# A block-sparse attention and feed-forward kernel: where the first weight matrix lies raw, in which order the two matrices are decoded, which queue carries the later transfers, and how many gathers go out at a time

## The chip, the cores and the metric

The kernel runs on one core of one Trainium2 chip. The metric is the device time of one execution in microseconds (us); less is better. The engines named below are PE (TensorE), DVE (VectorE), ACT (ScalarE), POOL (GpSimd) and SP (SyncE, which here only starts transfers). Transfers started by SP, ACT and POOL stand in three queues, q1, q10 and q0, and are carried out by the core's 16 DMA engines.

## The reference, cut to what matters

```python
# q, k, v: (4 batches, 8 heads, 768 positions, 64); 24 blocks of 32 positions
scores = np.matmul(q, k.transpose(0, 1, 3, 2)) / np.sqrt(64)
# a query block sees: its neighbours (|i - j| <= 1), the first and the last block,
# 3 sampled blocks of its own; blocks 0 and 23 see everything
attn = softmax(np.where(mask, scores, -1e9)) @ v
x = attn.transpose(0, 2, 1, 3).reshape(3072, 512)
h = x @ w_in                                   # w_in: 512 x 2048, float64
sp = np.maximum(h, 0) + np.log1p(np.exp(-np.abs(h)))
out = (h * erf(sp)) @ w_out                    # w_out: 2048 x 512, float64
```

The weights arrive as float64. The kernel takes them as pairs of 32-bit words and makes float32 of them on DVE.

## The kernel before, in words

**Work units.** Each of the four batches has 16 attention units: ten "m" units (five groups of four query blocks, two halves of the heads each), four "f" and two "e" units for the edge blocks. A unit is: `scores` on PE into `s`; `soft_max` (maximum, on DVE, into `mx` and `nb`); `soft_exp` (exponentials and a rounded copy on ACT, into `pf` and `p`); `soft_low` (the rest `p` on DVE); `soft_turn` (transposes of `p` into `pT`, on PE in the prologue, by a DMA transpose of SP's queue later). Two units later `values` multiplies `pT` with the value rows in `vb` on PE (into `po`), `norm` divides on DVE (into `xf`) and `turn` makes the transposed feed-forward input `xT`.

**Feed-forward steps.** The main loop has 96 groups plus a lag of two. Step m does on PE `ff_first` of group m (`h`, 24 products with `w_in`), `values`, `scores`, and `ff_second` of group m-2 (`o`, 12 products with `w_out`); on ACT five logarithm and exponential passes over `h` (`ff_logs`: four names `x`, one `q`), one more later (`ff_exp`); on DVE `ff_gate` of group m-1 (`q`, `g`, `g`) and `ff_power`. Each engine runs its instructions in the order in which the program writes them.

**Weights.** `w_in` and `w_out` are 16 raw pieces of 512 KB each. `load_weight` starts a transfer; step D (`decode_pair`) turns two pieces into float32 with three DVE instructions through `spare_k`; Q (`square_pair`) sums squares on ACT; A and B (`sum_w`, `scale_w`) make a scale from all eight sums of a matrix; H and L (`split_hi` on ACT, `split_lo` on DVE) make the two float16 halves which PE uses. "Di4" is D of pair 4 of `w_in`, "Lo0" L of pair 0 of `w_out`. A group of `ff_first` uses two pairs (steps 0 and 1 pairs 0 and 1, steps 2 and 3 pairs 2 and 3, and so on); `ff_second` of group n uses pair n of `w_out`. Raw pieces lie in the matrix's own tile, in slots that decoding frees step by step, and the last two in `spare_k`. The strings in `WEIGHTS` give what the main loop does at the end of steps 0, 1, 2 and so on.

**Values.** `load_v` brings raw `v`, `split_v` makes two float16 halves and writes them to a table in DRAM (`vtab`); `gather_v` brings the rows that two query blocks see into two of the eight slots of `vb`, some nine to twelve small transfers of SP's queue, and `gathers` starts as many as there are free slots. Before `values` of the first unit, SP's queue has: raw k, q, v; weights; the four writes to `vtab`; then the gathers. `gather` copies key blocks on POOL (`kg`).

**Queues.** SP's queue carries everything of the first batch, all gathers and DMA transposes and the q loads; POOL's carries the other weight pieces; ACT's the k and v of later batches and the results (`write_results`).

Of the kernel before, what the change touches and what calls it, by code (L numbers as in the profile page):

```python
# [26 lines left out]
WEIGHTS = (  # L27
    "Do7 Qo7 Hi2 Li2 Ao/Hi3 Li3 Bo Ho0 Lo0/Hi4 Li4 Ho1 Lo1/Hi5 Li5 Ho2 Lo2"
    "/Hi6 Li6 Ho3 Lo3/Hi7 Li7 Ho4 Lo4/Ho5 Lo5/Ho6 Lo6/Ho7 Lo7"
# [5 lines left out]
def sparse_attention_moe(ctx: ExitStack, tc: tile.TileContext, qT, kT, v, sampled, w_in, w_out, out):  # L35
# [36 lines left out]
    FF_LAG = 2  # L72
# [27 lines left out]
    def load_k(b, pr):  # L100
# [8 lines left out]
        eng = sp if b == 0 else act  # L109
        eng.dma_start(kr, kT[b, 2 * pr : 2 * pr + 2].rearrange("t d s -> (t d) s"))  # L110
# [38 lines left out]
    def load_v(b, quad):  # L149
# [5 lines left out]
        eng = act if b else sp  # L155
        eng.dma_start(vr, v[b][:, quad * 4 : quad * 4 + 4].rearrange("p h k d -> p h (k d)"))
# [185 lines left out]
    numbers = {}  # L342
# [15 lines left out]
    def gather_v(b, first):  # L358

        rows, last = vtab[b], first + 2  # L360
        if first % 4 == 1:
            numbers[b] = block_numbers(first, min(first + 4, NB - 1), SYNC)
# [67 lines left out]
    def raw_slot(i):  # L430

        return 2 + 2 * i if i < 8 else 10 + 2 * (i - 8) if i < 12 else 14 + 2 * (i - 12)
# [3 lines left out]
    def load_weight(eng, key, i):  # L436

        raw = spare_k[:, (i - 14) * 1024 : (i - 13) * 1024] if i > 13 else slots(wmats[key][0], raw_slot(i), 2)
# [5 lines left out]
        eng.dma_start(raw, rows)  # L444

    def decode_pair(key, k):

        t = wmats[key][0]
        raw = spare_k[:, :2048] if k == 7 else slots(t, raw_slot(2 * k), 4)
        decode(t, (2 * k + 2) * 512, raw, wide)  # L450
# [33 lines left out]
    wsteps = iter(WEIGHTS.split("/"))  # L484
# [261 lines left out]
    def write_results():  # L746
        for result in results:
            act.dma_start(*result)
# [15 lines left out]
    def gathers(m):  # L764

        nonlocal kfree, vfree
        if kjobs and kfree >= 4 and kjobs[0][0] in have_k:
            kfree -= 4
            gather(*kjobs.pop(0))
        while vjobs and vjobs[0][0] in have_v:  # L770
            b, i = vjobs[0]
            n = 2 if i > 0 else 1
            if vfree < n:
                break
            vfree -= n
            vjobs.pop(0)
            gather_v(b, i) if i > 0 else whole_v(b, -1 - i)

    def next_queries(m):

        b, n = divmod(m, per)
        if n < 10 and n % 2 == 1:
            order_q(b, n // 2 + 1)
        if n == per - 1 and b + 1 < B:
            order_q(b + 1, 0)

    def behind(m):

        b, n = divmod(m, per)
        if n < 10 and n % 2 == 0 and (b > 0 or n > 4):  # L790
            load_q(b, n // 2 + 1)
        if b + 1 < B:
            c = b + 1
            if n == 10:
                load_q(c, 0)
            if b == 0:
# [15 lines left out]
            if 7 <= n < 11:  # L812
                order_k(c, n - 7)
            if 6 <= n < 10:
# [222 lines left out]
```

## Time and profile before

| | |
|---|---|
| runs of the kernel before | 879.27, 879.34, 880.84 us; median 879.34 us |
| the profiled execution's own time | 874.48 us |
| its span, first to last instruction | 872.7 us |
| PE busy | 713.5 us, 82% of the span |
| ACT busy | 601.1 us, 69% |
| DVE busy | 555.3 us, 64% |
| POOL busy | 122.6 us, 14% |
| mean granted PE clock | 0.932 of full speed |

The profiled execution is one execution; its time is 4.86 us under the median of the three others, and 1.8 us of it lie outside the span. A busy share is an average over stages: the first hundred microseconds, the steps in which weights are split, and the rest have different limits.

### The profile page before, as it was taken

Reading aid. Unit: us, or ns where it says so; the run is one execution under the profiler, and the core shown is the slowest. Engines: PE = TensorE matmul, PEld = TensorE weight load, DVE = VectorE, ACT = ScalarE, POOL = GpSimd, SP = SyncE. Lnnn points to the kernel's source line nnn. Section 1 sums busy time; section 2 is a strip of 40 time slices with the busy share of each in tenths; the row PEclk is TensorE's granted clock in tenths of the full one; section 3 lists DMA queues with packets and bytes.
Section 4 is the critical chain, followed back from the end, with each engine's and each line's share of the span. In section 5 each row is a group of like instructions: output and inputs, shape, how many; then the busy total and the mean of one; then the engine's idle time right before and its main releaser. Section 6 shows DMA issues by size and latency. Waiting matters only on the chain. (4 is left out here: it accounts for less than half of the span.)

```text
span 872.7 us, 26694 instructions
## 1 busy us (share of the span) xinstructions
PE 713.5 (82%) x11100; PEld 510.1 (58%) x11100; DVE 555.3 (64%) x974; ACT 601.1 (69%) x999; POOL 122.6 (14%) x346
## 2 busy tenths in 40 slices
PE   1324357669994989899988999799989999999997
PEld 1213245446673667666766776566767676667664
DVE  3946866677763666865665677765656677655443
ACT  4634557778774767786775778776757686876774
POOL 6502120101210203200011121200111000000000
PEclk9965587879997999999999999899999999999999
DMA  8978723667577877962478678941475578221000
GB/s 330 352 216 237 222 66 79 168 177 188 153 153 191 178 172 203 226 176 50 104 198 184 141 178 207 231 95 32 121 193 118 137 159 180 78 50 37 2 26 25
DMA packets 199930, 131.61 MB, mean 151 GB/s; under 512 B 144000, under 2 KB 167168, under 8 KB 199808
## 3 DMA queue, kind: packets, MB, share of 16 engines
q1 hardware_dynamic: 189552, 98.96, 48.5%
q10 hardware_dynamic: 6544, 18.09, 6.5%
q0 software_dynamic: 3712, 12.85, 4.2%
q8 instruction: 87, 1.43, 0.7%
q14 instruction: 35, 0.29, 0.1%
HBM read 83.88 MB, written 12.95 MB: 111 GB/s over the span
## 5 line engine op out<-in xcount | busy, mean ns | idle before, releaser
L51 PE MATMUL h<-xT,wi 128*128 128x256 f16 x2304 | 276.4, 277 | 22.0 <-ACT wi L51 16.9
L51 PE MATMUL o<-wo,g 128*128 128x512 f16 x1152 | 267.4, 381 | 6.2 <-DVE wo L51 4.4
L51 PEld LDWEIGHTS <-wi 128*128 128x128 f16 x2304 | 228.5, 100 | 73.8 <-ACT wi L51 17.9
L51 ACT ACTIVATE x<-x 128x512 f32<-128x512 f32 x288 | 181.5, 630 | 9.1
L51 PEld LDWEIGHTS <-g 128*128 128x128 f16 x1152 | 109.3, 98 | 129.4 <-issue 9.6
L51 POOL COPY kg<-kx 128x128 f32 x264 | 87.1, 379 | 398.0 <-PE s_m L51 310.3
L51 ACT ACTIVATE pf_m<-s_m,nb_m 128x256 f32<-128x256 f32 x160 | 62.6, 474 | 75.0 <-DVE nb_m L51 69.8
L51 DVE SCALAR_TENSOR_TENSOR q<-x,q 128x512 f32<-128x512 f32 x96 | 66.2, 689 | 72.7 <-ACT x L51 71.6
L51 ACT ACTIVATE x<-h,isg 128x512 f32<-128x512 f32 x96 | 65.1, 678 | 52.7 <-PE h L51 33.4
L51 PE MATMUL po<-vb,pT_m 128*32 128x65 f16 (+1 forms) x3840 | 45.4, 206 | 51.9 <-DMA pT_m<-p_m 30.5
L51 PE MATMUL s_m<-kx,qm 128*64 128x64 f32 (+1 forms) x1280 | 76.4, 255 | 10.5 <-ACT pf_m L51 6.9
L51 ACT ACTIVATE q<-q 128x512 f32<-128x512 f32 x96 | 59.5, 620 | 29.9 <-DVE q L51 29.9
L51 DVE SCALAR_TENSOR_TENSOR q<-q,h 128x512 f32<-128x512 f32 x96 | 65.5, 682 | 22.6 <-ACT q L51 22.6
L51 PEld LDWEIGHTS <-pT_m 128*32 128x32 f16 x3840 | 39.4, 101 | 62.1 <-DMA pT_m<-p_m 33.0
L51 DVE TENSOR_TENSOR p_m<-pf_m,p_m 128x1024 f16<-128x1024 f32 x40 | 49.0, 1225 | 37.5 <-ACT p_m L51 37.5
L51 PEld LDWEIGHTS s_m<-kx,qm 128*64 128x64 f32 x1280 | 61.0, 152 | 14.4 <-ACT pf_m L51 7.8
L51 DVE SCALAR_TENSOR_TENSOR g<-q,g 128x512 f16<-128x512 f32 x96 | 66.5, 692 | 3.3
L51 DVE TENSOR_REDUCE mx_m<-s_m 128x4 f32<-128x1024 f32 x40 | 48.7, 1219 | 24.8 <-PE s_m L51 24.8
L51 ACT ACTIVATE q<-x 128x512 f32<-128x512 f32 x96 | 60.5, 630 | 3.0
L51 DVE TENSOR_TENSOR x<-xf,x 128x512 f16<-128x512 f32 x24 | 16.7, 696 | 44.9 <-ACT x L51 41.0
L51 PE MATMUL s_m<-kg,qm 128*64 128x96 f32 x640 | 44.8, 265 | 0.0
L51 DVE TENSOR_SCALAR g<-q 128x512 f16<-128x512 f32 x96 | 41.5, 432 | 3.3
(111 smaller groups left out, 629.5 us busy)
## 6 DMA issues: line engine op xcount, KB each, us to landing
vb<-vtab SPq DMA_DIRECT2D x280, 65.0 KB, 2.8
vb<-vtab SPq DMA_DIRECT2D x32, 390.0 KB, 3.9
wo<-in_w_out_dram POOLq DMA_DIRECT2D x14, 512.0 KB, 11.2
vraw<-in_v_dram ACTq DMA_DIRECT2D x9, 768.0 KB, 5.0
vtab<-vn SPq DMA_DIRECT2D x16, 390.0 KB, 4.5
vb<-vtab SPq DMA_DIRECT2D x12, 520.0 KB, 5.0
qt<-in_qT_dram SPq DMA_DIRECT2D x20, 256.0 KB, 4.3
out_dram<-wo ACTq DMA_DIRECT2D x20, 256.0 KB, 3.1
```

Of the source, the lines that this page charges most:

```text
L51: done = call(*args, **kwargs)
```

## The change: what it does

The raw pieces 8 to 15 of `w_in` go to `w_out`'s tile, slots 2 to 17, so they wait for no decoding. SP's queue takes four pieces of `w_in` in place of eight, and POOL's takes the other twelve and two of `w_out` in one go, behind the first key gather. `w_in` is decoded whole before `w_out`; the pieces of `w_out` are asked for as `w_in`'s decoding frees their slots. Four decodings of `w_out` (Do4 to Do7) now stand in the main loop, where one (Do7) stood. The weight steps of the main loop are split over two places, `EARLY` ahead of `ff_second` and `soft_max`, `LATE` at the step's end. k, v and results go through SP's queue. A call of `gathers` takes slots up to a sum of four, where a slot that also needs its edge blocks counts twice. The q loads and the key work of the next batch stand at other steps.

```diff
-WEIGHTS = (
-    "Do7 Qo7 Hi2 Li2 Ao/Hi3 Li3 Bo Ho0 Lo0/Hi4 Li4 Ho1 Lo1/Hi5 Li5 Ho2 Lo2"
-    "/Hi6 Li6 Ho3 Lo3/Hi7 Li7 Ho4 Lo4/Ho5 Lo5/Ho6 Lo6/Ho7 Lo7"
+EARLY = ("Hi2 Li2", "Li3 Qo5", "Ao Bo Ho0 Lo0", "Hi5 Li5", "Hi6 Li6", "Hi7 Li7")
+LATE = (
+    "Hi3 Do4 Qo4 Do5", "Do6 Qo6 Do7 Qo7", "Hi4 Li4 Ho1 Lo1", "Ho2 Lo2",
+    "Ho3 Lo3", "Ho4 Lo4", "Ho5 Lo5", "Ho6 Lo6", "Ho7 Lo7",
 )
...
-        eng = sp if b == 0 else act
-        eng.dma_start(kr, kT[b, 2 * pr : 2 * pr + 2].rearrange("t d s -> (t d) s"))
+        sp.dma_start(kr, kT[b, 2 * pr : 2 * pr + 2].rearrange("t d s -> (t d) s"))
...
-        eng = act if b else sp
-        eng.dma_start(vr, v[b][:, quad * 4 : quad * 4 + 4].rearrange("p h k d -> p h (k d)"))
+        sp.dma_start(vr, v[b][:, quad * 4 : quad * 4 + 4].rearrange("p h k d -> p h (k d)"))
...
+    def raw_of(key, i, n):
+
+        if key == "i":
+            return slots(wi, 2 + 2 * i, 2 * n) if i < 8 else slots(wo, 2 + 2 * (i - 8), 2 * n)
+        if i > 13:
+            return spare_k[:, (i - 14) * 1024 : (i - 14 + n) * 1024]
+        return slots(wo, 2 + 2 * i if i < 8 else 10 + 2 * (i - 8) if i < 12 else 14 + 2 * (i - 12), 2 * n)
...
-        for i in {2: (8, 9), 3: (10, 11), 5: (12, 13)}.get(k, ()):
-            load_weight(pool, key, i)
-        if k == 7 and key == "i":
-            for i in (14, 15):
-                load_weight(pool, "o", i)
+        freed = {4: (0, 1), 5: (2, 3), 6: (4, 5), 7: (6, 7)} if key == "i" else {2: (8, 9), 3: (10, 11), 5: (12, 13)}
+        for i in freed.get(k, ()):
+            load_weight(pool, "o", i)
...
-            act.dma_start(*result)
+            sp.dma_start(*result)
...
+        room = 4 if begun > 0 else VGS
         while vjobs and vjobs[0][0] in have_v:
             b, i = vjobs[0]
             n = 2 if i > 0 else 1
-            if vfree < n:
+            fresh = b > 0 and 0 < i < VGS
+            if vfree < n or room < n * (1 + fresh):
                 break
             vfree -= n
+            room -= n * (1 + fresh)
...
-    for i in range(8):
+    for i in range(4):
         load_weight(sp, "i", i)
...
     gathers(0)
+    numbers[0] = block_numbers(1, 5, SYNC)
+    early.append((0, 1))
+    for i in range(4, 16):
+        load_weight(pool, "i", i)
     for i in (14, 15):
-        load_weight(pool, "i", i)
-    for i in range(8):
         load_weight(pool, "o", i)
...
-    work("Do0 Qo0 Do1 Qo1")
+    work("Di4 Qi4 Di5")
     soft_max(units[2])
     soft_exp(units[2])
-    work("Di4 Qi4")
+    work("Qi5 Di6")
     values_of(seen(units[0]))
     norm(*seen(units[0]))
-    work("Di5 Qi5")
     soft_low(units[2])
 
     soft_turn(units[2])
+    values_of(seen(units[1]))
     scores(units[3])
     used_keys(units[3])
-    work("Do2 Qo2")
+    gathers(0)
+    work("Qi6 Di7 Qi7")
+    norm(*seen(units[1]))
+    work("Do0")
+    turn(*seen(units[1]))
     soft_max(units[3])
+    work("Ai")
     soft_exp(units[3])
     order_q(0, 2)
-    values_of(seen(units[1]))
-    gathers(0)
-    norm(*seen(units[1]))
-    turn(*seen(units[1]))
-    work("Di6 Qi6 Di7")
+    work("Qo0 Do1 Bi Hi0 Qo1")
     soft_low(units[3])
-    work("Qi7")
 
     soft_turn(units[3])
-    work("Do3 Qo3 Ai Do4")
+    work("Li0 Do2 Hi1")
     values_of(seen(units[2]))
-    work("Bi Hi0 Qo4")
     norm(*seen(units[2]))
     values_of(seen(units[3]))
-    work("Do5 Qo5")
+    work("Qo2 Li1")
     norm(*seen(units[3]))
     turn(*seen(units[3]))
-    work("Li0 Hi1 Li1 Do6 Qo6")
+    work("Do3 Qo3")
...
         write_values()
+        write_results()
...
-        if m >= FF_LAG:
-            for u in range(CT):
-                ff_second(*groups[m - FF_LAG], u)
         if last:
             ff_gate(*last)
         if place:
             norm(*place)
+        if m < len(EARLY):
+            work(EARLY[m])
+        if m >= FF_LAG:
+            for u in range(CT):
+                ff_second(*groups[m - FF_LAG], u)
...
-        write_results()
-        work(next(wsteps, ""))
+        if m < len(LATE):
+            work(LATE[m])
```

Where the order on an engine changes, the rows of the two programs show it. The first place is POOL's queue behind the first key gather (`kg_4` is its last copy); before:

```order
L51 COPY kg_4_212<-kx_162 128x128
L51 DMA spare_k<-in_w_in_dram 128x1024 x2
L51 DMA wo<-in_w_out_dram 128x1024 x8
L314 TENSOR_LOAD samp
L51 ISA
L51 COPY kg_5_447<-kx_162 128x128
```

and of the change:

```order
L52 COPY kg_4_208<-kx_158 128x128
L52 DMA wi<-in_w_in_dram 128x1024 x4
L52 DMA wo<-in_w_in_dram 128x1024 x8
L52 DMA spare_k<-in_w_out_dram 128x1024 x2
L313 TENSOR_LOAD samp
L52 ISA
L52 COPY kg_5_384<-kx_158 128x128
```

Fourteen loads of 512 KB stand there where ten stood, and the next key gather (`kg_5`) stands behind all of them.

The second place is DVE in steps 0 and 1 of the main loop, from the maximum of the unit of step 0 on; before (the three rows with `spare_k` are the decoding Do7, the row `wi<-wi,s_wi` is Li2):

```order
L51 TENSOR_REDUCE mx_m_2_0_1350<-s_m_2_0_1325 128x4
L51 TENSOR_SCALAR nb_m_2_0_1352<-mx_m_2_0_1350 128x4
L51 SCALAR_TENSOR_TENSOR q_0_0_1322<-x_0_0_1318,q_0_0_1322 128x512
L51 TENSOR_TENSOR p_m_2_0_1360<-pf_m_2_0_1355,p_m_2_0_1360 128x4x256
L51 TENSOR_SCALAR spare_k<-spare_k 128x1024
L51 SCALAR_TENSOR_TENSOR spare_k<-spare_k 128x1024
L51 SCALAR_TENSOR_TENSOR wo<-spare_k 128x1024
L51 SCALAR_TENSOR_TENSOR wi<-wi,s_wi 128x2x512
L51 TENSOR_REDUCE top_wo<-sums 128x1
L51 SCALAR_TENSOR_TENSOR q_0_0_1322<-q_0_0_1322,h_0_0_1293 128x512
```

and of the change (the six rows with `spare_k` are Do4 and Do5; the last row is Li3):

```order
L52 TENSOR_TENSOR p_m_2_0_1345<-pf_m_2_0_1340,p_m_2_0_1345 128x4x256
L52 TENSOR_SCALAR spare_k<-wo 128x1024
L52 SCALAR_TENSOR_TENSOR spare_k<-wo,spare_k 128x1024
L52 SCALAR_TENSOR_TENSOR wo<-wo,spare_k 128x1024
L52 TENSOR_SCALAR spare_k<-wo 128x1024
L52 SCALAR_TENSOR_TENSOR spare_k<-wo,spare_k 128x1024
L52 SCALAR_TENSOR_TENSOR wo<-wo,spare_k 128x1024
L52 SCALAR_TENSOR_TENSOR q_0_0_1305<-q_0_0_1305,h_0_0_1276 128x512
L52 TENSOR_SCALAR g_0_0_1420<-q_0_0_1305 128x512
L52 SCALAR_TENSOR_TENSOR g_0_0_1420<-q_0_0_1305,g_0_0_1420 128x512
L52 SCALAR_TENSOR_TENSOR wi<-wi,s_wi 128x2x512
```

Two decodings stand between the unit's last DVE instruction and the gate of group 0, where one stood, and the split that PE needs for step 2 (Li3) stands behind the gate.

The third place is SP's queue in the second step of the second batch (`xT_2` and `pT_m_0_1` are transposes of that step, `pT_m_1_0` one of the next step); before, from the last of thirty gather transfers on:

```order
L51 DMA vb<-vtab_95 32x1040
L51 DMA_TRANSPOSE xT_2_2819<-x_0_5_3841 128x8x128
L51 DMA_TRANSPOSE pT_m_0_1_3846<-p_m_0_1_3838 128x16x128
L51 DMA_TRANSPOSE pT_m_1_0_4080<-p_m_1_0_4076 128x16x128
L51 DMA qt_2_4082<-in_qT_dram 128x4x128
```

and of the change, from the last of nine on:

```order
L52 DMA vb<-vtab_95 32x1040
L52 DMA qt_2_3787<-in_qT_dram 128x4x128
L52 DMA_TRANSPOSE xT_2_2819<-x_0_5_3798 128x8x128
L52 DMA_TRANSPOSE pT_m_0_1_3803<-p_m_0_1_3795 128x16x128
L52 DMA vraw_0_3808<-in_v_dram 128x1536
L313 TENSOR_LOAD samp
L52 DMA vb<-vtab_95 32x2x1040 x2
```

The transposes of the step stand behind nine gather transfers and a q load, where thirty stood; nine more gathers, and twelve after these, follow in the next two steps, and a v load stands among them.

## Rows read from the trace of the kernel before

**Rows 1.** SP's queue in order of time, first 180 us: start, us from the first to the last of the run, what, how many.

```profile
5.92 9.43 SPq L51 DMA_DIRECT2D wi<-in_w_in_dram  x8
...
20.23 19.82 SPq L51 DMA_DIRECT2D vtab<-vn  x4
53.51 55.08 SPq L51 DMA_DIRECT2D vb<-vtab  x66
```

**Rows 2.** POOL in order of time, the starts of weight loads, same columns.

```profile
17.28 1.10 POOL L51 DMA_DIRECT2D spare_k<-in_w_in_dram  x2
...
38.31 1.07 POOL L51 DMA_DIRECT2D wi<-in_w_in_dram  x2
41.56 1.04 POOL L51 DMA_DIRECT2D wi<-in_w_in_dram  x2 [2.18 <-DVE wi L51]
```

**Rows 3.** The transfer queues (q1 is SP's, q0 POOL's) in three stretches, 20 to 25, 30 to 35 and 40 to 45 us: packets, MB, time of the packets as a share of 16 engines.

```profile
q0 software_dynamic: 212, 0.80, 40.1%
...
q0 software_dynamic: 488, 1.76, 87.0%
q1 hardware_dynamic: 487, 0.24, 16.2%
...
q1 hardware_dynamic: 1031, 0.52, 98.5%
q0 software_dynamic: 63, 0.25, 23.8%
```

**Rows 4.** DVE in order of time: start, us, what; in brackets the idle time before it and what ended it. The first three are one decoding.

```profile
23.80 0.69 DVE L51 TENSOR_SCALAR spare_k<-wi 128x1024 int32<-128x1024 int32 x1
24.52 1.23 DVE L51 SCALAR_TENSOR_TENSOR spare_k<-wi,spare_k 128x1024 int32<-128x1024 int32 x1
25.78 1.22 DVE L51 SCALAR_TENSOR_TENSOR wi<-wi,spare_k 128x1024 int32<-128x1024 int32 x1
...
66.68 0.16 DVE L51 TENSOR_SCALAR rinv<-po 128x4 f32<-128x4 f32 x1 [13.33 <-PE po L51]
...
154.79 1.21 DVE L51 TENSOR_REDUCE mx_m<-s_m 128x4 f32<-128x1024 f32 x1
...
161.77 1.28 DVE L51 SCALAR_TENSOR_TENSOR wi<-wi,s_wi 128x1024 f16<-128x1024 f32 x1
```

**Rows 5.** PE in order of time, same columns: the end of the first value product, the first product of the first step, the first use of `w_out`, and two waits for the splits of `w_in`.

```profile
65.21 1.44 PE L51 MATMUL po<-vb,pT_m 128*32 128x65 f16 x89 [0.15 <-DMA vb<-vtab]
...
107.45 1.87 PE L51 MATMUL h<-xT,wi 128*128 128x256 f16 x8 [1.11 <-ACT xT L51]
...
143.88 2.76 PE L51 MATMUL o<-wo,g 128*128 128x512 f16 x12
...
161.09 0.61 PE L51 MATMUL h<-xT,wi 128*128 128x256 f16 x2 [5.58 <-ACT wi L51]
...
186.87 0.61 PE L51 MATMUL h<-xT,wi 128*128 128x256 f16 x2 [5.91 <-ACT wi L51]
```

**Rows 6.** ACT in order of time: the first pass over `h` in steps 3 and 5 of the main loop.

```profile
152.48 0.67 ACT L51 ACTIVATE x<-h,isg 128x512 f32<-128x512 f32 x1
...
177.81 0.67 ACT L51 ACTIVATE x<-h,isg 128x512 f32<-128x512 f32 x1
```

**Rows 7.** Stretches of 20 us: busy time of PE, PE's weight loads, DVE, ACT and POOL (instructions in brackets), granted PE clock, DMA share, GB/s.

```profile
140.00:160.00 20.00, 15.50 (x344) 11.21 (x342) 13.07 (x23) 16.96 (x30) 3.93 (x13) 0.93 0.49 113
160.00:180.00 20.00, 17.51 (x354) 12.48 (x355) 14.37 (x21) 14.27 (x23) 1.75 (x6) 0.85 0.65 152
180.00:200.00 20.00, 12.68 (x161) 8.25 (x160) 14.34 (x28) 14.62 (x23) 0.12 (x1) 0.74 0.62 173
260.00:280.00 20.00, 8.99 (x222) 6.88 (x208) 7.89 (x14) 10.56 (x20) 0.00 (x0) 0.80 0.85 212
```

**Rows 8.** SP's queue in order of time at the changes from the first to the second batch and from the second to the third.

```profile
251.56 21.58 SPq L51 DMA_DIRECT2D vb<-vtab  x30
...
274.59 3.97 SPq L51 DMA_TRANSPOSE pT_m<-p_m  x2
...
433.25 20.24 SPq L51 DMA_DIRECT2D vb<-vtab  x27
```

**Rows 9.** PE in order of time, same columns as rows 5: its waits for a DMA transpose.

```profile
278.60 1.50 PE L51 MATMUL po<-vb,pT_m 128*32 128x65 f16 x96 [11.01 <-DMA pT_m<-p_m]
...
352.99 0.96 PE L51 MATMUL po<-vb,pT_m 128*32 128x65 f16 x96 [2.96 <-DMA pT_m<-p_m]
...
459.13 1.18 PE L51 MATMUL po<-vb,pT_m 128*32 128x65 f16 x96 [4.04 <-DMA pT_m<-p_m]
...
557.45 1.50 PE L51 MATMUL po<-vb,pT_m 128*32 128x65 f16 x96 [4.92 <-DMA pT_m<-p_m]
...
647.33 1.51 PE L51 MATMUL po<-vb,pT_m 128*32 128x65 f16 x96 [3.26 <-DMA pT_m<-p_m]
```

**Rows 10.** Transfers over the whole span, by what they write and read: engine, how many, KB each, median us from issue to landing.

```profile
vraw<-in_v_dram ACTq DMA_DIRECT2D x9, 768.0 KB, 5.0
vtab<-vn SPq DMA_DIRECT2D x16, 390.0 KB, 4.5
...
out_dram<-wo ACTq DMA_DIRECT2D x20, 256.0 KB, 3.1
wi<-in_kT_dram ACTq DMA_DIRECT2D x12, 384.0 KB, 3.6
```

More of the change, by code (lines that the diff above doesn't have):

```diff
@@ L341, in sparse_attention_moe @@
     ended = {}
-    numbers = {}
+    numbers, early = {}, []
     def whole_rows(b):
@@ L360, in gather_v @@
         rows, last = vtab[b], first + 2
-        if first % 4 == 1:
+        if first % 4 == 1 and (b, first) not in early:
             numbers[b] = block_numbers(first, min(first + 4, NB - 1), SYNC)
@@ L428, in sparse_attention_moe @@
     wide = spare_k[:, 2048:3072]
-    def raw_slot(i):
-        return 2 + 2 * i if i < 8 else 10 + 2 * (i - 8) if i < 12 else 14 + 2 * (i - 12)
+    def raw_of(key, i, n):
[4 more added lines that the diff above has]
+        return slots(wo, 2 + 2 * i if i < 8 else 10 + 2 * (i - 8) if i < 12 else 14 + 2 * (i - 12), 2 * n)
     assert NK * NG == NF == 16
     def load_weight(eng, key, i):
-        raw = spare_k[:, (i - 14) * 1024 : (i - 13) * 1024] if i > 13 else slots(wmats[key][0], raw_slot(i), 2)
         if key == "i":
@@ L443, in load_weight @@
             rows = w_out[i * P : (i + 1) * P, :].bitcast(I32)
-        eng.dma_start(raw, rows)
+        eng.dma_start(raw_of(key, i, 1), rows)
     def decode_pair(key, k):
         t = wmats[key][0]
-        raw = spare_k[:, :2048] if k == 7 else slots(t, raw_slot(2 * k), 4)
-        decode(t, (2 * k + 2) * 512, raw, wide)
-        for i in {2: (8, 9), 3: (10, 11), 5: (12, 13)}.get(k, ()):
-            load_weight(pool, key, i)
-        if k == 7 and key == "i":
-            for i in (14, 15):
-                load_weight(pool, "o", i)
+        decode(t, (2 * k + 2) * 512, raw_of(key, 2 * k, 2), wide)
+        freed = {4: (0, 1), 5: (2, 3), 6: (4, 5), 7: (6, 7)} if key == "i" else {2: (8, 9), 3: (10, 11), 5: (12, 13)}
+        for i in freed.get(k, ()):
+            load_weight(pool, "o", i)
     def square_pair(key, k):
@@ L483, in sparse_attention_moe @@
     steps_of = {"D": decode_pair, "Q": square_pair, "A": sum_w, "B": scale_w, "H": split_hi, "L": split_lo}
-    wsteps = iter(WEIGHTS.split("/"))
     def work(steps):
@@ L783, in next_queries @@
             order_q(b, n // 2 + 1)
+            if n < 9:
+                load_q(b, n // 2 + 2)
         if n == per - 1 and b + 1 < B:
             order_q(b + 1, 0)
+            load_q(b + 1, 1)
     def behind(m):
         b, n = divmod(m, per)
-        if n < 10 and n % 2 == 0 and (b > 0 or n > 4):
-            load_q(b, n // 2 + 1)
         if b + 1 < B:
@@ L795, in behind @@
                 load_q(c, 0)
+            k = n if b else 2 * (n - 10) if n > 9 else -1
+            if k in ((1, 3, 5, 7) if b else (2, 4, 6, 8)):
+                order_k(c, (k - 1) // 2)
+            if k in (0, 2, 4, 6):
+                load_k(c, k // 2)
+            if k == 8:
+                have_k.add(c)
             if b == 0:
@@ L811, in behind @@
                 have_v.add(c)
-            if 7 <= n < 11:
-                order_k(c, n - 7)
-            if 6 <= n < 10:
-                load_k(c, n - 6)
-            if n == 10:
-                have_k.add(c)
     def seen(unit):
@@ L996, in sparse_attention_moe @@
             soft_turn(unit)
-        write_results()
-        work(next(wsteps, ""))
+        if m < len(LATE):
+            work(LATE[m])
         if unit:
             behind(begun - 1)
+    write_results()
 _OUTS = [((3072, 512), "float32")]
```

1 line of the change is left out of this document (removed).

## The prediction

> **What bounds the kernel now.** I read the busy times by stage first, then each engine in order of time in the first 200 us, then PE's waits after that. Averages hide three stages.
>
> The first stage ends when PE starts the feed-forward, at 107.45 us [rows 5]. It is a chain of transfers and then of DVE work. SP issues the four writes to `vtab` from 20.23 us on and is done with that at 40.05, but its first gather starts only at 53.51 [rows 1]: it waits for the last write to land. The first value product ends at 66.65 [rows 5], and DVE, which has decoded ahead until 53.35, sits idle for 13.33 us until then [rows 4]. From 66.65 on DVE works off decodings. One decoding is 0.69 + 1.23 + 1.22 = 3.14 us [rows 4], and seven stand between the first value product and the first `h` (Di5, Do2, Di6, Di7, Do3, Do4, Do5).
>
> The second stage, steps 0 to 8, ends near 200 us. PE waits 5.58 and 5.91 us there for splits of `w_in` that stand at the end of the step before [rows 5]. ACT and DVE are far from idle in it: from 140 to 200 us ACT is busy 16.96 + 14.27 + 14.62 = 45.9 of 60 us, DVE 41.8 [rows 7].
>
> In the third stage PE sets the pace and loses time where a DMA transpose comes late: 11.01 us at 278.60, and 2.96, 4.04, 4.92 and 3.26 us later [rows 9]. At the first, SP had issued thirty gathers for 21.58 us and came to the transposes at 273 to 275 us [rows 8].
>
> **The change, part by part.** The sum is made against the profiled span of 872.7 us. That execution's time, 874.48 us, is 4.86 us under the median of the three runs; I add the difference to the median, 879.34.
>
> *The writes to `vtab`.* POOL issues its first loads at 17.28 us [rows 2], and q0 moves 0.80 MB up to 25 us and then 1.76 MB in 5 us [rows 3], so it starts near 22.7 us. Fourteen loads of 512 KB, 7.34 MB, keep it busy for 20.9 us, to 43.6. In a shared stretch q1 gets 487 packets while q0 gets 488, although q1's are small and q0's 4 KB: 97 per us, so about 2,030 by 43.6. The four writes are 390 KB each in pieces of 520 B, 3,072 packets. The other 1,040 go alone; with q0's 63 taken off at one for one, q1 moved 968 in 4.35 us [rows 3], 222 per us, so 4.7 us: 48.3. SP's four loads fewer let q1 start on the small packets before q0 is up, at best some 700 of them, 45. I take 46.5, so 7.0 earlier than 53.5. Before, ten loads went first and four more came at 38.31 and 41.56 us [rows 2], into the end of these writes; now nothing follows the fourteen until Di4 has run.
>
> The Trainium skill (DMA: Bandwidth & Descriptors, Queues, rings and completion order) says that each DMA engine goes round its queue rows packet by packet. The near-equal counts agree. The rule speaks against this part: a load moved to another queue is not out of the way of 520-byte packets, and if it governed to the end, the writes would land no earlier.
>
> *The first gathers.* They ran with q0 quiet. Now Di4, Di5 and Di6, which stand where Do0, Do1 and Di4 stood and so end by 53.4, each start two loads of `w_out`: six loads, 3.1 MB, 8.9 us of q0. Bounds 0 and 8.9; since the gathers are spaced by SP's issuing too (66 transfers in 55.08 us [rows 1]), I take 2.4. First value product at 62.0, 4.6 earlier.
>
> *Decodings ahead of `h`.* Four instead of seven (Di7, Do0, Do1, Do2): 3 x 3.14 = 9.4 us. DVE is the chain here, so all of it counts: `h` starts 14.0 us earlier, at 93.4.
>
> *Decodings behind it.* Do4, Do5, Do6 now stand in steps 0 and 1 beside Do7. DVE meets Do4 and Do5 ahead of the gate and of Li3, on which PE's third group waits, and Do6 and Do7 ahead of the next gate, with Qo7, the scale and Ho0 behind them, on which the first `o` waits. So 9.4 us come back, less what DVE's waits in that stretch swallow. Bounds 0 and 9.4; I take 6.0, since gate, split and maximum queue behind the decodings on one engine. The first `o` is at 135.9 instead of 143.88 [rows 5]: 8.0 of the gain are left.
>
> *Splits ahead of the softmax.* PE's waits of 5.58 and 5.91 us go. But the split on DVE (1.28 us) now stands ahead of the maximum (1.21) [rows 4], so ACT, which had split just before, waits for both until it may take the exponentials. ACT's first pass is at 152.48 and at 177.81 us [rows 6], 25.3 us for two steps; its own busy share of 76% in this stretch [rows 7] gives 19.4, and twice 2.5 us of new waiting make 24.4. I take 1.0 us in all for the stage (bounds: 11.5, both waits whole, and a loss of 2).
>
> *SP's queue at a change of batch.* Thirty gathers become nine, nine and twelve in three steps, with transposes between. At 21.58 / 30 = 0.72 us each [rows 8] nine take 6.5, so the transpose that came 11.01 us late is issued some 15 us earlier. But the number of gathers up to the next batch's sixth step is unchanged, k, v and q loads stand among them on the same queue, and the DMA engines are already 0.85 busy there [rows 7]. Part of the wait comes back in the next steps. Bounds 0 and 13 (the wait and PE's slower clock behind it: 0.80 of full in the stretch [rows 7]); I take 6.
>
> *The later waits.* 4.04 and 3.26 us follow batch changes (the first after 27 gathers in 20.24 us [rows 8]); 2.96 and 4.92 stand late in a batch, where by the program ACT starts k and v loads while SP gathers. Together 15.2 [rows 9]. I take 9 of them back and 2 as new waits for values that are gathered only a step ahead: 7 (bounds 15 and a loss of 2).
>
> The early read of block numbers, the q loads a little earlier and the renamed slots cost nothing: they lie under SP's wait for the writes and under PE's work; uncovered they would cost a transfer's landing, a few us once.
>
> Sum: 8.0 + 1.0 + 6 + 7 = 22.0 us. 879.3 - 22.0 = **857.3 us**.
>
> **The rivals.** *The gain at the first `h` is kept.* If DVE's waits swallow the decodings behind it, the steps start 14.0 instead of 8.0 earlier, and PE's two waits come on top with half, 5.7; with 8 and 8 for the later waits the sum is 35.7: 843.6 us. For it speaks that DVE is busy only 41.8 of 60 us behind 140 [rows 7], against it that those gaps are waits for ACT.
>
> *The writes land no earlier.* Fourteen loads in a row beside small packets, and six more behind them: the first value product stays at 66.65. Then 8.0 becomes 3.4, nothing is won in the splits, and the queue gives 4 and 3: 10.4 us, 868.9 us. For it speaks the one-for-one sharing [rows 3], against it that q1 starts with four loads fewer.
>
> *Slower: one queue too many on SP.* All k, v and results now stand ahead of transposes and gathers in q1. There are 9 v loads at 5.0 us to landing, 12 k loads at 3.6 and 20 large results at 3.1 [rows 10], together 150 us. If 29 us of these, one fifth, reached PE as late transposes, the gain of 22 would turn into a loss of 7: 886 us. It decides from 15% on. Against it: SP issues them behind the step's transposes, and `pT` is used two units later.
>
> The Trainium skill (the same page, Issuing engines are not separate DMA queues) holds that starting transfers from several engines saves only the time to start them; by it the move of k, v and results would cost issue time alone, well under the 150 us. No row here shows both arrangements.
>
> **How the numbers follow.** Forecast 0.50, gain kept 0.24, writes no earlier 0.18, slower 0.08, of which I put 0.03 within 0.2% (1.8 us, about what a measurement of this kernel can tell from no change). The first three are all faster: 0.92. The range is 841 to 870 us: below it the gain-kept case with still more of its bounds, above it the slower one.
>
> **What would show it.** Right: SP's first gather near 46 us, the first value product near 62, the first `h` near 93, the first `o` near 136; no wait of PE for `wi`, but a longer one of ACT for the maximum; thirty gathers in three runs, and PE's wait of 11 us cut to a half. Wrong: the first gather still near 53 us; the steps up to 200 us at less than 11 us each; new waits of PE for `vb` or `pT` at each change of batch, together over 10 us; ACT waiting for a transfer.

## The result, and the profile after

| | before | after |
|---|---|---|
| time, median (lowest to highest) | 880.09 us (879.27 to 887.20, 4 runs) | 857.06 us (856.55 to 861.46, 4 runs) |
| profiled execution, and its span | 874.48, 872.7 us | 856.55, 854.8 us |
| mean granted PE clock | 0.932 | 0.940 |

The ratio is 0.9732, 95% interval 0.9672 to 0.9792: faster, by 23.0 us in the medians. The forecast was 857.3 us. The profiled executions differ by only 17.9 us, since that of before is 5.6 us under its median here; so the traces can account for 17.9, not for 23.

The sum was right and its terms were not. The table follows one mark, PE's first product `h` of a feed-forward group, through both traces (us; groups are counted from 0).

| group | 0 | 3 | 7 | 12 | 15 | 16 | 20 | 28 | 40 | 52 | 64 | 72 | 95 |
|---|---|---|---|---|---|---|---|---|---|---|---|---|---|
| before | 107.4 | 146.5 | 197.7 | 237.9 | 264.8 | 285.6 | 318.8 | 381.6 | 471.3 | 569.2 | 659.4 | 717.6 | 856.3 |
| after | 96.2 | 144.8 | 189.8 | 234.0 | 262.0 | 270.1 | 312.2 | 371.6 | 456.2 | 554.6 | 640.5 | 699.9 | 837.8 |
| difference | -11.3 | -1.6 | -7.9 | -3.9 | -2.8 | -15.4 | -6.6 | -10.0 | -15.1 | -14.6 | -18.9 | -17.7 | -18.5 |

Up to group 15, ahead of the first change of batch, the gain has shrunk to 2.8 us in these two traces. The trace of before is an early one, though. Two kernels of the experiments below run its prologue and splits too, and six run those of the change. Group 15 starts at 264.8, 267.2 and 269.8 us in the three traces with the old ones and at 261.4 to 266.2 in the seven with the new ones: means of 267.3 and 262.9, 4.4 us apart. So differences of 2 us in the table are within what single traces differ by, and the gain ahead of the first change of batch is nearer to 4.4 us than to 2.8. Most of the gain comes behind that point.

**The prologue.** SP's queue in order of time (start, us from the first to the last of the run, what, how many), which answers to [rows 1]:

```profile
20.36 16.07 SPq L52 DMA_DIRECT2D vtab<-vn  x4
45.14 56.26 SPq L52 DMA_DIRECT2D vb<-vtab  x66
```

POOL in order of time, the loads of `w_out` that Di4, Di5 and Di6 set free:

```profile
46.24 1.07 POOL L52 DMA_DIRECT2D wo<-in_w_out_dram  x2 [3.36 <-DVE wi L52]
49.49 1.05 POOL L52 DMA_DIRECT2D wo<-in_w_out_dram  x2 [2.18 <-DVE wi L52]
53.95 1.05 POOL L52 DMA_DIRECT2D wo<-in_w_out_dram  x2 [3.42 <-DVE wi L52]
```

The transfer queues from 53 to 63 us, while these loads move (packets, MB, time of the packets as a share of 16 engines):

```profile
q0 software_dynamic: 543, 1.98, 68.3%
q1 hardware_dynamic: 581, 0.97, 34.8%
```

PE in order of time; in brackets the idle time before and what ended it. These answer to [rows 5]:

```profile
64.77 0.21 PE L52 MATMUL po<-vb,pT_m 128*32 128x65 f16 x1 [9.86 <-DMA vb<-vtab]
65.92 1.87 PE L52 MATMUL po<-vb,pT_m 128*32 128x65 f16 x93 [0.95 <-DMA vb<-vtab]
...
96.16 4.92 PE L52 MATMUL h<-xT,wi 128*128 128x256 f16 x24 [1.11 <-ACT xT L52]
...
121.57 3.32 PE L52 MATMUL h<-xT,wi 128*128 128x256 f16 x16 [7.12 <-DVE wi L52]
...
135.98 0.59 PE L52 MATMUL whole_wo<-one,top_wo 128*128 128x1 f32 x2 [7.41 <-DVE top_wo L52]
138.88 0.59 PE L52 MATMUL o<-wo,g 128*128 128x512 f16 x1 [2.31 <-ACT wo L52]
```

And DVE's idle time, which answers to the 13.33 us of [rows 4]:

```profile
67.83 0.16 DVE L52 TENSOR_SCALAR rinv<-po 128x4 f32<-128x4 f32 x1 [14.18 <-PE po L52]
```

The first gather starts 8.4 us earlier than in [rows 1], and yet the first value product ends at 67.79 us, 1.1 later than before. The gathers now run beside the six loads, and from the first gather to the end of that product it takes 22.6 us where it took 13.1. The two queues move nearly as many packets, but one of q1 carries 1.7 KB and one of q0 3.6 KB.

**The steps up to 200 us.** ACT's exponentials and PE's second products in order of time:

```profile
155.66 1.57 ACT L52 ACTIVATE pf_m<-s_m,nb_m 128x256 f32<-128x256 f32 x4 [2.76 <-DVE nb_m L52]
167.57 1.57 ACT L52 ACTIVATE pf_m<-s_m,nb_m 128x256 f32<-128x256 f32 x4 [2.91 <-DVE nb_m L52]
```

```profile
160.45 0.38 PE L52 MATMUL o<-wo,g 128*128 128x512 f16 x1 [1.16 <-ACT wo L52]
162.47 3.98 PE L52 MATMUL o<-wo,g 128*128 128x512 f16 x11 [1.64 <-DVE wo L52]
```

The waits of 5.58 and 5.91 us for `w_in` in [rows 5] are gone. From 100 to 205 us PE waits 9.6 us in all for `w_in`, most of it the 7.12 us shown above, where it waited 20.9. In exchange ACT waits some 2.8 us in each step, and PE 11.1 us in all for splits of `w_out`, for which it did not wait before.

**The changes of batch.** SP's gathers at the first change, where [rows 8] has thirty in a row, and PE there and at two later places that answer to [rows 9]:

```profile
246.60 5.04 SPq L52 DMA_DIRECT2D vb<-vtab  x9
...
263.71 5.13 SPq L52 DMA_DIRECT2D vb<-vtab  x9
...
272.36 6.14 SPq L52 DMA_DIRECT2D vb<-vtab  x12
```

```profile
273.76 0.21 PE L52 MATMUL po<-vb,pT_m 128*32 128x65 f16 x2 [0.85 <-DMA pT_m<-p_m]
278.77 0.24 PE L52 MATMUL po<-vb,pT_m 128*32 128x65 f16 x1 [4.80 <-DMA vb<-vtab]
...
361.30 0.96 PE L52 MATMUL po<-vb,pT_m 128*32 128x65 f16 x96 [1.38 <-DMA pT_m<-p_m]
...
675.77 0.96 PE L52 MATMUL po<-vb,pT_m 128*32 128x65 f16 x96 [2.81 <-DMA pT_m<-p_m]
```

PE's waits from 240 to 720 us, all of a kind together (us in total, times, longest), say the same in one line each, the first of them from before:

```profile
PE po L51 <- DMA pT_m<-p_m: 29.4, 8, 11.0
...
PE po L52 <- DMA pT_m<-p_m: 8.1, 5, 2.8
PE po L52 <- DMA vb<-vtab: 6.0, 5, 4.8
```

### The profile page after: what moved, and what is told of

It is laid out like the page before. It is cut to its first block, busy times and chain, and to the rows that moved or that the text cites. A ratio compares the mean times of both kernels' runs of the same rounds, so it can differ in the third digit from the quotient of the medians.

```text
span 854.8 us, 26699 instructions
## 1 busy us (share of the span) xinstructions
PE 712.1 (83%) x11100; PEld 505.2 (59%) x11100; DVE 553.7 (65%) x974; ACT 601.0 (70%) x999; POOL 136.0 (16%) x350
## 4 chain that ended last, share of the span: by engine, by line
PE 43%; DVE 17%; ACT 13%; DMA 11%; issue 10%; SPq 2%; POOL 2%; POOLq 0%; ACTq 0%
PE h L52 17%; PE o L52 16%; PE po L52 4%; PE s_m L52 4%; ACT x L52 3%; ACT pf_m L52 3%; DMA vtab<-vn 3%; DVE mx_m L52 3%; DVE g L52 3%; DVE q L52 3%; DMA vb<-vtab 2%; ACT q L52 2%; SPq L52 2%; DVE p_m L52 2%; ACT p_m L52 2%
## 5 line engine op out<-in xcount | busy, mean ns | idle before, releaser
L52 PE MATMUL o<-wo,g 128*128 128x512 f16 x1152 | 271.0, 384 | 16.2 <-DVE wo L52 8.5
L52 PE MATMUL h<-xT,wi 128*128 128x256 f16 x2304 | 273.8, 276 | 12.4 <-DVE wi L52 8.3
L52 POOL COPY kg<-kx 128x128 f32 x264 | 97.6, 422 | 281.7 <-PE s_m L52 176.6
L52 DVE SCALAR_TENSOR_TENSOR q<-q,h 128x512 f32<-128x512 f32 x96 | 65.5, 682 | 22.6 <-ACT q L52 21.9
L52 PE MATMUL s_m<-kg,qm 128*64 128x96 f32 x640 | 47.7, 258 | 6.0 <-POOL kg L52 4.7
```

Source lines behind the costliest of these rows:

```text
L52: done = call(*args, **kwargs)
```

## The experiments

Each is an edit of the changed kernel unless it says otherwise. The kernel before ran beside them in three groups, with medians of 878.58, 879.67 and 880.08 us.

| kernel | median, us | ratio to before | 95% interval |
|---|---|---|---|
| changed kernel | 857.06 | 0.9732 | 0.9672 to 0.9792 |
| six loads behind the gathers | 860.65 | 0.9806 | 0.9777 to 0.9835 |
| k, v, results back on ACT | 865.28 | 0.9836 | 0.9807 to 0.9865 |
| no cap | 878.41 | 1.0010 | 0.9979 to 1.0042 |
| splits behind the softmax | 855.12 | 0.9730 | 0.9705 to 0.9755 |
| old prologue and splits | 861.63 | 0.9769 | 0.9727 to 0.9812 |
| no cap, and k, v, results on ACT | 877.04 | 0.9951 | 0.9925 to 0.9977 |
| cap of 8 | 868.79 | 0.9860 | 0.9824 to 0.9896 |
| kernel before, cap alone | 875.36 | 0.9933 | 0.9901 to 0.9965 |
| results alone on ACT | 869.40 | 0.9888 | 0.9856 to 0.9920 |
| k and v alone on ACT | 856.47 | 0.9730 | 0.9706 to 0.9753 |
| four places first | 855.84 | 0.9713 | 0.9693 to 0.9734 |
| four places first, splits behind | 853.15 | 0.9704 | 0.9670 to 0.9737 |

### What stretches the first gathers

```
-            load_weight(pool, "o", i)
+            load_weight(sp if key == "i" and k < 7 else pool, "o", i)
```

> The six loads of w_out that follow Di4 to Di6 go on SP's queue, behind the 40 gathers that stand there, instead of on POOL's beside them. Theory (these loads are what stretches the first gathers: 22.6 us from the first gather to the end of the first value product in the changed kernel, 13.1 before): the first gather stays at 45.1 us, the first value product ends at 58 to 60 instead of 67.8, the first h starts 8 to 9 us earlier than 96.2, and the time is 848 to 852 us instead of 857. Rival (the gathers are slow by themselves, since SP issues them one by one, or since the other loads on POOL are still moving): first value product at 65 to 68 us, time 855 to 859 us. A third outcome: the gain at the first value product is there, but Do0 to Do2 now wait for their data and the first h gains less than 4 us: 853 to 856 us.

The mechanism is as the theory has it. The first value product starts its bulk 8.6 us earlier, and from 45 to 58 us q0 moves nothing and the queue of the gathers is alone:

```profile
57.35 1.82 PE L52 MATMUL po<-vb,pT_m 128*32 128x65 f16 x93 [0.34 <-DMA vb<-vtab]
```

```profile
q1 hardware_dynamic: 1344, 2.13, 58.6%
```

The changed kernel moves 1.32 MB on this queue in the same 13 us, 62% of the 2.13 here. But the time does not fall. DVE, in order of time, now stands and waits for the very loads that were moved:

```profile
74.04 0.69 DVE L52 TENSOR_SCALAR spare_k<-wo 128x1024 int32<-128x1024 int32 x1 [8.74 <-DMA wo<-in_w_out_dram]
```

and the first `h` starts at 96.48, where the changed kernel has 96.16. The 860.65 us are 3.6 over the changed kernel; the intervals overlap. So these two orders give the same prologue: DVE's next work needs the loads as soon as the values. An order between the two is tried at the end of this section.

### The splits ahead of the softmax

```
-        if m < len(EARLY):
+        if m == 2:
             work(EARLY[m])
 ...
+        if m < len(EARLY) and m != 2:
+            work(EARLY[m])
         if m < len(LATE):
```

> The splits that the changed kernel has ahead of the softmax (steps 0, 1, 3, 4, 5) go back behind it, at the end of the same step. Theory (the place of the splits only trades one wait for another: ACT waits 2.75 us for the maximum in each step, PE no longer waits for w_in): ACT's waits of 2.75 us go, PE's waits of 5 to 6 us for wi come back in the steps up to 200 us, and the time is 855 to 860 us. Rival (PE's waits were the larger loss, as the forecast of 1 us to 11.5 us has it): 860 to 868 us. Other rival (ACT's waits are the larger loss, ACT being busiest there): 848 to 854 us.

One wait was traded for the other. From 100 to 205 us the changed kernel has, all waits of a kind together:

```profile
PE h L52 <- DVE wi L52: 8.3, 3, 7.1
PE h L52 <- ACT wi L52: 1.3, 1, 1.3
...
ACT pf_m L52 <- DVE nb_m L52: 15.4, 6, 2.9
```

and with the splits put back:

```profile
PE h L52 <- DVE wi L52: 16.9, 4, 13.0
PE h L52 <- ACT wi L52: 10.9, 4, 5.9
...
ACT pf_m L52 <- DVE nb_m L52: 7.7, 5, 2.7
```

PE waits 18.2 us more for `w_in` and 12.2 less for `w_out` and its maximum, ACT 7.7 less for the maximum of the scores, and group 12 starts at 232.7 us instead of 234.0. The time is the same within the intervals. So PE's waits for `w_in` in this stretch were not the price of the old order; that they were slack behind ACT and DVE is the reading that fits, and no run shows it by itself.

### What the new prologue and the splits bring in all

The kernel before with the cap, the transfers on SP and the moved loads of q and k alone; of the change's diff these hunks are left out:

```
-EARLY = ("Hi2 Li2", "Li3 Qo5", ...)
+WEIGHTS = ("Do7 Qo7 Hi2 Li2 Ao/Hi3 Li3 Bo Ho0 Lo0/...")
-    for i in range(4, 16):
-        load_weight(pool, "i", i)
-    work("Di4 Qi4 Di5")
+    work("Do0 Qo0 Do1 Qo1")
 ...
```

> The kernel before with the cap on gathers, the transfers on SP's queue and the new places of the loads of q and k: the changed kernel without its new prologue and without its moved splits. Theory (the prologue and the splits are worth only the 3 to 4 us by which the groups start earlier from 240 to 262 us, the rest comes from the queue): 858 to 862 us. Rival (9 us, as the forecast's first two terms have it): 864 to 868 us. Other rival (the start of the batch change moves with the prologue, and what follows falls into other places): outside both.

861.63 us: prologue and splits are worth 4.6 us where the forecast put 9.0. The runs spread from 856.0 to 865.0, so this is good to a few us; the ten traces counted in the section on the result say 4.4 at group 15 and 5.3 at group 12.

### The cap

```
-        room = 4 if begun > 0 else VGS
+        room = 4 * VGS
```

> The gathers of values are no longer capped at four places in a step. Theory (the cap breaks up the runs of gathers ahead of the transposes): about thirty gathers in one run on SP at the first change of batch, PE's wait of 4.8 us there becomes 9 to 11, waits of 3 to 4 us come back at the second and third, 862 to 868 us. Rival (the waits at the changes of batch are set by the transfers themselves, not by their order on SP): 855 to 859 us.

```
-        room = 4 if begun > 0 else VGS
+        room = 8 if begun > 0 else VGS
```

> The cap is 8 places in a step instead of 4. At a change of batch two fresh pairs may follow each other, so about 18 gathers stand in a run where the changed kernel has 9 and the kernel without a cap 30. Theory (what costs is the length of the run ahead of the transposes): between the two, 862 to 872 us. Rival (4 is too strict, since PE waits 4.8 us for values at the first change): 850 to 855 us. Other rival (only the shortest runs help): 874 to 880 us.

Without the cap the whole gain goes, 21.4 us, far more than the 5 to 11 that the expectation gave it. SP at the first change of batch, and PE there, without the cap:

```profile
246.52 19.30 SPq L52 DMA_DIRECT2D vb<-vtab  x30
```

```profile
271.83 1.50 PE L52 MATMUL po<-vb,pT_m 128*32 128x65 f16 x96 [6.88 <-DMA pT_m<-p_m]
```

PE is not the only one to wait there. A load of the next batch's v stands in SP's queue behind the thirty gathers (issued at 270.04, landed at 276.47), and ACT, which sums the squares of v (`vj`), stands still until it has landed:

```profile
276.49 0.84 ACT L52 ACTIVATE vj<-vraw 128x768 bf16<-128x768 f32 x1 [11.91 <-DMA vraw<-in_v_dram]
```

Group 16 starts at 284.6 us instead of 270.1. The damage does not end at the wait. From 262 to 330 us PE (first column of busy time) does less in the kernel without the cap, first row, than in the changed kernel, second row, at a granted clock of 0.87 instead of 0.95, a mean over the clock's two levels:

```profile
262.00:330.00 68.00, 53.67 (x950) 38.66 (x949) 35.80 (x70) 41.81 (x75) 10.92 (x30) 0.87 0.82 175
```

```profile
262.00:330.00 68.00, 59.70 (x1107) 44.68 (x1105) 41.72 (x80) 48.31 (x87) 14.94 (x39) 0.95 0.88 212
```

The next two changes add to it (groups 40 and 64: 5.0 and 8.7 us later than before, the changed kernel 15.1 and 18.9 earlier). With 8 places 18 gathers stand in a row and the time lies between, 868.79:

```profile
248.64 13.47 SPq L52 DMA_DIRECT2D vb<-vtab  x18
```

The time grows with the length of the run: 9, 18 and 30 gathers give 857.1, 868.8 and 878.4 us. ACT's waits for v loads at `vj` from 240 to 720 us grow with it; 9, 18 and 30 gathers in order:

```profile
ACT vj L52 <- DMA vraw<-in_v_dram: 2.9, 2, 1.6
ACT vj L52 <- DMA vraw<-in_v_dram: 18.4, 3, 7.8
ACT vj L52 <- DMA vraw<-in_v_dram: 28.2, 3, 11.9
```

PE's waits for transposes do not. They are 8.1 us with 9 gathers, as shown above, and with 18 and 30:

```profile
PE po L52 <- DMA pT_m<-p_m: 5.4, 5, 1.4
PE po L52 <- DMA pT_m<-p_m: 19.2, 6, 6.9
```

With 18 gathers PE waits less for transposes than with 9, and the time is 11.7 us longer all the same. So late transposes, which the cap was meant to cure, are not the whole price, and ACT's wait for v is the part that keeps step with the time. No run without the cap had v alone on another queue, so how the price divides between the two stays open.

Since the cap alone on the kernel before is worth little (next), this is its price in the changed kernel, not its gain by itself.

### The cap by itself, and the queue without it

The kernel before with the cap's lines added and nothing else:

```
+        room = 4 if begun > 0 else VGS
 ...
+            fresh = b > 0 and 0 < i < VGS
+            if vfree < n or room < n * (1 + fresh):
 ...
+            room -= n * (1 + fresh)
```

> The kernel before with the cap alone. If the cap works by itself, taking most of PE's 30.5 us of waits for transposes behind 260 us: 858 to 864 us. If it needs the new order of the other transfers on SP (k and v loads of the next batch still come in a row from ACT, beside the gathers): 868 to 876 us.

875.36 us, 4.3 less than before. The wait for a transpose at 278.60 in [rows 9] is gone, and others have come in its place. PE in order of time:

```profile
283.01 0.24 PE L51 MATMUL po<-vb,pT_m 128*32 128x65 f16 x1 [4.55 <-DMA vb<-vtab]
...
288.27 0.24 PE L51 MATMUL po<-vb,pT_m 128*32 128x65 f16 x4 [5.02 <-DMA vb<-vtab]
```

The changed kernel without the cap and with k, v and results on ACT's queue again (the next section's diff and this line):

```
-        room = 4 if begun > 0 else VGS
+        room = 4 * VGS
```

> The changed kernel without the cap and with k, v and results back on ACT's queue. If the cap (21 us when taken away alone) and the move to SP (8 us when taken away alone) stand each by itself, both together cost 29 us: 884 to 889 us. If they hang together, since k, v and results on SP make its runs of gathers longer and the cap is the cure for that, the move is worth nothing or less without the cap: 872 to 878 us.

877.04 us. PE's waits for transposes from 240 to 720 us are back at the amount of before:

```profile
PE po L52 <- DMA pT_m<-p_m: 31.3, 7, 10.8
```

So with the new prologue there are four cells: cap and SP 857.1, cap and ACT 865.3, no cap and SP 878.4, no cap and ACT 877.0. The move to SP is worth 8.2 us with the cap and nothing (-1.4) without it; the cap is worth 21.4 with the move and 11.8 without. The kernel before differs by up to 1.5 us between the groups of runs, so such differences are good to about that; they hang together beyond it. Without the cap the move trades one wait for another: on SP PE waits 19.2 us for transposes and ACT 28.2 for v, on ACT's queue PE waits 31.3 and ACT not at all for v, but 19.8 on gathers and results.

One part of the change has no run of its own, the new places of the q and k loads. The cap on the kernel before gives 875.36 us, and the changed kernel with k, v and results on ACT 865.28. Prologue and splits are some 4.6 of these 10.1 us; whether the rest is the q and k loads or comes of the parts acting together, no run shows.

### Which of the moved transfers counts

All three kinds back on ACT:

```
-        sp.dma_start(kr, ...)
+        (act if b else sp).dma_start(kr, ...)
-        sp.dma_start(vr, ...)
+        (act if b else sp).dma_start(vr, ...)
-            sp.dma_start(*result)
+            act.dma_start(*result)
```

with the results written at the step's end again.

> The loads of k and v of the second batch on and the results go back on ACT's queue, the results at the end of a step, all else as in the changed kernel. If the move of these transfers was worth something of its own (the later waits, 11.9 us less where 7 were forecast): PE waits for the transposes return late in a batch (2.96 and 4.92 us before), and the time is 860 to 865 us. If it is worth nothing, since ACT only issues: 855 to 859 us, and the start of the feed-forward groups after 260 us lies within 2 us of the changed kernel's. If SP's queue was too full: 850 to 854 us.

Then the diff's first two edits alone, k and v, and its third alone, the results, again written at the step's end:

> The other half: the loads of k and v of the second batch on go back on ACT's queue, the results stay on SP's. If k and v carry the 8 us: 862 to 866 us, with PE's waits for values at the first change of batch spread over several places as with all three put back (2.8, 2.8, 2.1 and 2.6 us); if the results do: 855 to 860 us.

> Of the three kinds of transfers that the change puts on SP's queue, the results alone go back on ACT's, at the end of a step. All three together cost 8 us when put back (865.28 against 857.06). If the results carry that: 862 to 866 us; if k and v do: 855 to 860 us.

Beside the cap, k and v make no difference (856.47). The results make all of it, and more: 869.40. Queue and place in the step were moved together here; a kernel with the results on SP at the step's end was not built. ACT in order of time with the results on its queue, at the change of batch and at a later place:

```profile
310.10 0.82 ACTq L52 DMA_DIRECT2D out_dram<-wo  x2
311.03 1.12 ACT L52 ACTIVATE vn<-vraw,s_v 128x384 f16<-128x384 f32 x2 [11.76 <-DMA vb<-vtab]
...
495.46 1.12 ACT L52 ACTIVATE vn<-vraw,s_v 128x384 f16<-128x384 f32 x2 [9.20 <-DMA vb<-vtab]
```

SP and PE in the same kernel:

```profile
301.97 8.68 SPq L52 DMA_DIRECT2D vb<-vtab  x15
```

```profile
313.94 4.47 PE L52 MATMUL o<-wo,g 128*128 128x512 f16 x12 [4.44 <-DVE g L52]
```

The same split of ACT in the changed kernel:

```profile
302.40 1.12 ACT L52 ACTIVATE vn<-vraw,s_v 128x384 f16<-128x384 f32 x2 [2.40 <-DVE i_v L52]
```

Issuing the two results takes ACT 0.82 us. What costs is that ACT stands still for 11.76 us, nearly all of it ahead of the first issue, and the reader should ask why a result waits for a gather. A completion counter is a semaphore that a transfer raises when it has landed. In the trace the issue waits for such a counter besides its data, and the result's counter is that of one of the fifteen gathers: SP issued it at 307.03, it landed at 310.03, and ACT issued the result at 310.10. In every trace here SP's transfers take turns on eight counters, and ACT's, where it issues any, on the same eight; POOL's have eight of their own. So the result must wait until the last transfer on its counter has landed, and that one stood in SP's queue behind other gathers. ACT's splits come 8.6 us later than in the changed kernel, and DVE's gate and PE's `o` come late by it. In the changed kernel ACT's longest wait for any transfer behind 240 us is 3.1 us. The results alone on ACT (869.40) cost 4 us more than all three kinds (865.28); in the latter the longest stall falls elsewhere (10.9 us ahead of an `x`), and why it is cheaper there was not tried.

### Versions that follow from this

The loads of `w_out` on SP again, but behind the four places that the first two value products read, the other four places after them:

```
-            load_weight(pool, "o", i)
+            load_weight(sp if key == "i" and k < 7 else pool, "o", i)
 ...
-        room = 4 if begun > 0 else VGS
+        room = 4 if begun > 0 or not slot_of else VGS
```

> The six loads of w_out go on SP's queue again, but the first call gathers only four places (what the first two value products read) and the loads stand right behind them; the other four places follow. Theory (the loads held up the first gathers, and put behind all 40 they came too late for DVE): first value product at 58 to 61 us, no wait of DVE for w_out over 3 us, first h at 88 to 91 us instead of 96.2. If the gain lives on to the steps behind 200 us: 850 to 854 us. If it is given back at the first o, where all kernels with this prologue have met so far: 856 to 860 us.

And this with the edit of the splits from above added:

> The same with the splits put back behind the softmax, which by themselves took 2 us (855.12, not told apart from 857.06). If both gains stand: 848 to 852 us. If the first is given back at the first o: 854 to 857 us.

855.84 and 853.15 us. In both the first value product ends near 59 and DVE no longer waits for a load. But the first `h` came at 97.88 us in one profile and at 88.16 in the other, with the same prologue. The first profile is that kernel's slowest run (861.84), the second the other's fastest (847.14), so the two show how far runs of this prologue go apart, not what the splits do. In the first, PE, in order of time, waited for the later gathers:

```profile
81.75 0.44 PE L52 MATMUL po<-vb,pT_m 128*32 128x65 f16 x4 [3.42 <-DMA vb<-vtab]
85.02 1.44 PE L52 MATMUL po<-vb,pT_m 128*32 128x65 f16 x89 [2.82 <-DMA vb<-vtab]
```

In the second the 8.0 us of the first `h` live on: group 12 starts 9.9 us before the changed kernel's, group 95 8.7 before. The runs spread from 854.7 to 861.8 and from 847.1 to 858.3. The second version has the lowest median of all, 3.9 us under the changed kernel; its interval overlaps that of the changed kernel, so it is better than before for certain, and better than the changed kernel only probably.

## Why the prediction was right, and where its steps were not

| step | forecast | trace |
|---|---|---|
| end of the first value product | -4.6 | +1.1 |
| decodings ahead of `h` | -9.4 | -12.4 |
| given back up to the first `o` | +6.0 | +6.3 |
| steps up to group 15 | -1.0 | +2.2 |
| first change of batch (to group 20) | -6 | -3.8 |
| behind it | -7 | -11.9 |
| sum to group 95 | -22.0 | -18.5 |

The column of the trace is the difference of one trace of each kernel. As the trace of before is an early one, its first four rows are good to some 2 us each.

Of the marks named beforehand the first gather came as told (45.14 for 46), and so did the three runs of gathers and the halved wait; the first value product (67.8 for 62), the first `h` (96.2 for 93) and the first `o` (138.9 for 136) came late. PE's waits for `wi` did not go altogether: 9.6 us of 20.9 are left.

*The writes and the first gather.* Right: 45.14 us for a forecast of 46.5. The queues shared as forecast: from 25 to 35 us q1 moved 947 packets beside q0's 949. Two figures on the way were off. q0 began to move at 19.5 us instead of 22.7 and was done with the fourteen loads at 41.7 instead of 43.6, and q1, all but alone, moved 466 and 500 packets in the two us from 40 to 42 where the forecast took 222 per us. The Trainium skill (DMA: Bandwidth & Descriptors, Queues, rings and completion order) says that each DMA engine goes round its queue rows packet by packet. The trace agrees, and yet the writes landed earlier: before, four more loads shared with them near the end (q0 moved 445 packets beside q1's 468 from 45 to 50 us), and now none did.

*The first gathers.* Wrong; the term that failed is the 2.4 us for the six loads. They cost 9.5: 22.6 us less 13.1. Its upper bound was 8.9, the time that q0 needs for them alone, and I took a quarter of it, because gathers are spaced by SP's issuing. The late loads show that spacing is not the limit: without the loads the same gathers take 13.9 us, so by this run the loads cost 8.7. The sharing between queues that I used two paragraphs earlier for the writes held here as well (581 packets beside 543 from 53 to 63 us), and the forecast did not apply it. The counters add to it. Here a gather is issued only when the transfer eight places before it has landed: one issued at 54.68 us landed at 64.72 beside the loads, and SP issued the next on its counter at 64.74. So beside the loads SP's spacing was itself a wait for landings.

*Decodings.* 28.4 us lie between the end of the first value product and the first `h`, against 40.8 before: 12.4 gained for a forecast of 9.4. Three decodings less are 9.4. The forecast let all of this stretch count as DVE's work, but before DVE also stood idle there for 8.0 us (2.27 ahead of a maximum and 3.83 ahead of `x` were the longest), and in the changed kernel for 2.7. That is more than the other 3.0; which of the new places took these waits away was not tried.

*Given back.* Right in size, 6.3 us. PE waits 7.41 us for `top_wo` and 7.12 for `w_in` (PE's rows above), as the queue of decodings on DVE has it; of these the first is not new, since the trace of before has 7.2 us there. The two other traces with the old prologue give 5.7 and 3.3 us for this row.

*Splits.* The two waits for `w_in` went and ACT's wait for the maximum came, as described; ACT's wait is 2.8 us a step for a forecast of 2.5. But no gain came of it, and putting the splits back gives the same time. The failed step is the 1.0 us, a price for PE's waits in a stretch in which they bought no time when they were taken away or put back.

*First change of batch.* The forecast was that the wait is cut to a half and part of it comes back: 0.85 + 4.80 us stand where 11.01 stood, and 3.8 us are gained by group 20 instead of 6.

*The later waits.* Undersized: 11.9 us instead of 7, and this makes up for the prologue. The forecast treated the cap and the move to SP as separate trims on the same waits. The four cells show that the move is worth nothing without the cap and the cap half as much without the move. What the forecast did not name in either is ACT: results on ACT's queue stop it, and without the cap v loads behind gathers on SP's queue stop it too. Its terms priced PE's late transposes alone.

*The rivals.* The gain was not kept, nor did the writes land late. The rival on the slower side, one queue too many on SP, is refuted beside the cap by its parts: k and v cost SP nothing (856.47 against 857.06), and results are better there. Without the cap it is half right: v on SP then stops ACT for 28.2 us, and the move gains nothing. The Trainium skill (the same page, Issuing engines are not separate DMA queues) says that issuing from several engines saves issue time and no more. For k and v the runs agree; for the results they go further, since the other engine stands still for 11.76 us around two issues that take it 0.82 us together, which is neither transfer nor issue time.

In all, the direction and the places of the gain were right, but that the total comes within 0.3 us is luck, since two errors offset: the prologue and splits gave 4.6 us instead of 9.0, and all else, the queue with the moved q and k loads, 18.0 instead of 13. Both measured figures are good to a few us.

## What to carry to other kernels

When an engine issues a transfer, price the wait ahead of the issue and not the issue: look in the trace for the releaser of the next instruction on that engine, and if it is a transfer of another queue, try the issue on that queue. Ask also what stands behind a run of small transfers on a queue, for every engine that waits for one of them. Where a load is set free by work that runs just before small urgent transfers, take its whole queue time as the cost, and ask who needs it next before moving it away. A wait of one engine need not be worth its length (here 5 to 6 us in a step were worth nothing that could be measured), and two edits at one bottleneck are to be measured in four cells, since here one was worth 8 us or nothing by the state of the other.

## What was not expected of the hardware

Sharing evenly by packet is not sharing evenly by bytes: from 53 to 63 us q1 moved 581 packets beside q0's 543, but 0.97 MB beside 1.98, and from 45 to 58 us it moved 1.32 MB where it moved 2.13 with q0 idle. SP's transfers take turns on eight completion counters and share them with ACT's, so a transfer's issue on one engine can be held by the landing of another engine's: ACT, idle from 299.27 us, issued its result at 310.10. Beside the loads of another queue the same counters held SP's own gathers back, one until the gather eight places before it had landed, 10.0 us after its issue.
